# Units of one key block for all heads, loads in order of need, and v cast by DMA, in a fused attention and MLP kernel

## Chip, cores, metric

One core of one Trainium2 chip. The metric is device time in microseconds (us), the median of the runs. "Span" is the length of the one execution that the profiler recorded; it is some 0.3 to 3 us shorter than the median time. Engines are TensorE (PE; its weight loads PEld), VectorE (DVE), ScalarE (ACT), GpSimd (POOL) and SyncE (SP).

## The reference

Eight batches of causal attention with a window of 128 and ALiBi, eight heads of 64, 576 positions; its result is the input of an MLP with ELU (512 to 2048 to 512) over 4608 tokens.

```python
# q, k, v: (8 batches, 8 heads, 576, 64) f32
scores = (1 / 8) * q @ k^T                        # per batch and head
rel = pos_q - pos_k;  slope[h] = 2 ** -(h + 1)    # 8 heads
mask = (rel >= 0) & (rel < 128)
scores = where(mask, scores - slope[h] * abs(rel), -1e9)
attn = softmax(scores);  x = (attn @ v) as (4608 tokens, 512)
h = x @ w_in                                      # w_in (512, 2048)
g = where(h > 0, h, exp(min(h, 0)) - 1)
return g @ w_out                                  # w_out (2048, 512), f32
```

576 is four and a half blocks of 128. Each batch therefore has a last block, called block 4 here, of only 64 positions.

## The kernel before

The MLP is cut into 144 hidden pieces (128 x 512 results each, then ELU on ACT, POOL and DVE) and 144 output pieces (4 matmuls each). A slot of the schedule holds one hidden piece, one output piece and a share of the attention of a later batch. Scores are held transposed (keys on partitions). A unit of attention is half of the heads and half of the positions. Value matmuls of block 4 run on full tiles: columns 512 to 576 of EX, the upper half of key block 4 in VP and the end of KT are zeros.

```python
KT = [one([128, 2, 2, 640], F16, f"KT{i}") for i in range(2)]
EX = [one([128, 4, 576], F16, f"EX{i}") for i in range(4)]
...
for i in range(2):
    V.memset(VP[i][:, :, :, D:D + 1], 1.0)        # gives the softmax's sum
    V.memset(VP[i][64:128, 4, :, 0:D], 0.0)
    V.memset(KT[i][:, :, :, 576:640], 0.0)
for e in EX:
    V.memset(e[:, :, 512:576], 0.0)
...
def values(b, i, h2):
    ...
    parts = {0: [(e0, 0, 0)],
             1: [(e0, 256, 1), (e0, 128, 0)],
             2: [(e1, 0, 2), (e0, 384, 1)],
             3: [(e1, 256, 3), (e1, 128, 2)],
             4: [(e1, 384, 3), (e1, 448, 4)]}[i]
    a = ps_v.tile([128, 4, D + 1], F32, name="av", tag="av")
    for g in range(4):
        for j, (e, c, n) in enumerate(parts):
            nc.tensor.matmul(a[:, g, :], e[:, g, c:c + 128], VP[b % 2][:, n, 2 * g + h2, 0:D + 1],
                             start=j == 0, stop=j == len(parts) - 1)
```

The start: q and k of batch 0 first, then a weight, then v (uncast, by the SP queue, cast by GpSimd), then the other weights and batch 1.

```python
for g in range(4):
    load_qk(0, 1, g); load_qk(0, 0, g)
...
load_wi(0)
for n in range(5):
    load_v(0, n)
load_wi(1)
...
for i in (2, 3):
    load_wi(i)
for g in range(4):
    for w in (1, 0):
        load_qk(1, w, g)
```

The softmax here doesn't subtract the row's maximum and nothing guards it: scores larger than these inputs give would overflow.

Of the kernel before, what the change touches and what calls it, by code (L numbers as in the profile page):

```python
# [14 lines left out]
BIG = 30000.0  # L15
# [3 lines left out]
def kernel(  # L19
# [34 lines left out]
    TAB = one([128, 2, 4, 512], F16, "TAB")  # L54

    QT = [one([128, 2, 2, S], F16, f"QT{i}") for i in range(2)]
    KT = [one([128, 2, 2, 640], F16, f"KT{i}") for i in range(2)]
    VP = [one([128, 5, H, VW], F16, f"VP{i}") for i in range(2)]
    EX = [one([128, 4, 576], F16, f"EX{i}") for i in range(4)]
# [5 lines left out]
    st, vf = {}, {}  # L65
# [8 lines left out]
    def turn_qk(b, w, h2, dh):  # L74
        o = (QT, KT)[w][b % 2][:, h2, dh, 0:S].rearrange("p (n i j) -> p n j i", i=32, j=2)
        V.transpose(o, st[b][:, w, h2, :, :, 32 * dh:32 * dh + 32])  # L76

    def load_v(b, n):
        t = vf[b, n] = stage.tile([128, H, D], F32, name="vf", tag="vf", bufs=5)
        p = 128 if n < 4 else 64  # L80
        if b == 0:
            nc.gpsimd.memset(t[:, 0, 0:1], 0.0)
        nc.sync.dma_start(t[0:p, :, :], v[b, :, 128 * n:128 * n + p, :].rearrange("h p d -> p h d"))

    def cast_v(b, n):
        p = 128 if n < 4 else 64
        nc.gpsimd.tensor_scalar(  # L87
            out=VP[b % 2][0:p, n, :, 0:D], in0=vf.pop((b, n))[0:p, :, :],
            scalar1=1.0, scalar2=0.0, op0=ALU.mult, op1=ALU.add)

    def load_wi(i, n=1):
        c = slice(512 * i, 512 * i + 512 * n)
        nc.gpsimd.dma_start(w_in_sb[:, :, c], moe_w_in[:, c].rearrange("(c p) f -> p c f", p=128))

    def load_wo(i, n=1):
        nc.gpsimd.dma_start(
            w_out_sb[:, 4 * i:4 * i + 4 * n, :],
            moe_w_out[512 * i:512 * i + 512 * n, :].rearrange("(c p) d -> p c d", p=128))
# [3 lines left out]
    with tc.manual_schedule():  # L102


        row = one([128, 1], I32, "row")
        col = one([128, 128], I32, "col")
        rel = one([128, 512], I32, "rel")
        nc.gpsimd.iota(row, pattern=[[0, 1]], base=0, channel_multiplier=1)
        nc.gpsimd.iota(col, pattern=[[1, 128]], base=0, channel_multiplier=0)
        for g in range(4):  # L110
            load_qk(0, 1, g)
            load_qk(0, 0, g)
        for c, n in ((0, 256), (256, 192), (448, 64)):
            nc.gpsimd.iota(rel[:, c:c + n], pattern=[[1, n]], base=0, channel_multiplier=-1)
        load_wi(0)
        for n in range(5):
            load_v(0, n)
        load_wi(1)

        rowf = one([128, 1], F32, "rowf")  # L120
        V.tensor_copy(rowf, row)
        V.tensor_scalar(out=ident, in0=col, scalar1=rowf, scalar2=None, op0=ALU.is_equal)  # L122
        ra = one([128, 512], F32, "ra")
        for i in range(2):
            V.memset(VP[i][:, :, :, D:D + 1], 1.0)
            V.memset(VP[i][64:128, 4, :, 0:D], 0.0)
            V.memset(KT[i][:, :, :, 576:640], 0.0)
        for e in EX:
            V.memset(e[:, :, 512:576], 0.0)
        V.tensor_scalar(out=ra, in0=rel, scalar1=0.0, scalar2=BIG, op0=ALU.is_lt, op1=ALU.mult)  # L130
        V.tensor_tensor(out=ra, in0=ra, in1=rel, op=ALU.add)
        rb = one([128, 512], F32, "rb")
        V.tensor_scalar(out=rb, in0=ra, scalar1=127.0, scalar2=BIG, op0=ALU.is_gt, op1=ALU.mult)
        V.tensor_tensor(out=ra, in0=ra, in1=rb, op=ALU.add)
        for h2 in range(2):
            for g in range(4):
                nc.scalar.activation(TAB[:, h2, g, :], ra, AF.Exp,
                                     scale=-(2.0 ** (-8.0 * (2 * g + h2 + 1) / H)))



        avt, xnt, xps = {}, {}, {}

        def unit(b, k_):
            return EX[(4 * b + k_) % 4]

        def scores(b, k_):
            u, h2 = divmod(k_, 2)
            qt, kt = QT[b % 2], KT[b % 2]
            parts = ([(0, 0, 0, 256), (256, 1, 128, 256)] if u == 0 else  # L150
                     [(0, 2, 256, 256), (256, 3, 384, 192), (448, 4, 512, 64)])
            for o, kb, q0, n in parts:
                for dh in range(2):
                    for g in range(4):
                        r = slice(32 * g, 32 * g + 32)
                        nc.tensor.matmul(  # L156
                            sp[:, g, o:o + n], kt[r, h2, dh, 128 * kb:128 * kb + 128],
                            qt[r, h2, dh, q0:q0 + n], start=dh == 0, stop=dh == 1,
                            tile_position=(32 * g, 0))

        def expo(b, k_, g):
            nc.scalar.activation(unit(b, k_)[:, g, 0:512], sp[:, g, :], AF.Exp, scale=0.125)  # L162

        def weigh(b, k_, gp):
            u, h2 = divmod(k_, 2)
            e = unit(b, k_)[:, 2 * gp:2 * gp + 2, 0:512]
            if u == 0:
                for_ = lambda ap: ap
                e = e.rearrange("p g (a c) -> p g a c", a=2)
                t = TAB[:, h2, 2 * gp:2 * gp + 2, 0:256].unsqueeze(2).broadcast_to([128, 2, 2, 256])  # L170
            else:
                t = TAB[:, h2, 2 * gp:2 * gp + 2, :]
            V.tensor_tensor(out=e, in0=e, in1=t, op=ALU.mult)  # L173

        def values(b, i, h2):
            e0, e1 = unit(b, h2), unit(b, 2 + h2)
            parts = {0: [(e0, 0, 0)],
                     1: [(e0, 256, 1), (e0, 128, 0)],
                     2: [(e1, 0, 2), (e0, 384, 1)],
                     3: [(e1, 256, 3), (e1, 128, 2)],  # L180
                     4: [(e1, 384, 3), (e1, 448, 4)]}[i]
            a = ps_v.tile([128, 4, D + 1], F32, name="av", tag="av")
            for g in range(4):
                for j, (e, c, n) in enumerate(parts):
                    nc.tensor.matmul(a[:, g, :], e[:, g, c:c + 128], VP[b % 2][:, n, 2 * g + h2, 0:D + 1],  # L185
                                     start=j == 0, stop=j == len(parts) - 1)
            if (b, i) not in xnt:
                xnt[b, i] = work.tile([128, 4, 2, D], F16, name="xn", tag="xn", bufs=6)
            r = work.tile([128, 4], F32, name="rden", tag="rden", bufs=2)
            V.reciprocal(out=r, in_=a[:, :, D])  # L190
            V.tensor_tensor(out=xnt[b, i][:, :, h2, :], in0=a[:, :, 0:D],  # L191
                            in1=r.unsqueeze(2).broadcast_to([128, 4, D]), op=ALU.mult)

        def turn(b, i):
            n = 128 if i < 4 else 64
            o = (b * S + 128 * i) % RING
            x = xnt.pop((b, i)).rearrange("p g h d -> p (g h d)")
            if b:
                nc.sync.dma_start_transpose(out=xT[:, :, o:o + n], in_=x[0:n, :])
                return  # L200
            t = ps_o.tile([128, 4, 128], F16, name="xps", tag="op")
            for c in range(4):
                nc.tensor.transpose(t[:, c, :], x[:, 128 * c:128 * c + 128], ident)
            V.tensor_copy(xT[:, :, o:o + n], t[:, :, 0:n])


        hps, es, gs, ops = {}, {}, {}, {}
        width = lambda t: 128 if t < 1 else 256

        def place(t, j):  # L210
            w = width(t)
            sub, s_ = divmod(j, w // 32)
            return w, w * sub, s_ * (512 // w), 512 // w

        def hidden(t, j):
            w, c0, f0, nf = place(t, j)
            p = hps[t, j] = ps_h.tile([128, 512], F32, name="hp", tag="hp")
# [9 lines left out]
            e = es[t, j] = work.tile([128, 512], F32, name="e", tag="e")  # L227
            nc.scalar.activation(e, p, AF.Exp)  # L228
            nc.gpsimd.tensor_scalar(out=e, in0=e, scalar1=1.0, scalar2=0.0, op0=ALU.min, op1=ALU.max)  # L229

        def elu(t, j):
            w, c0, f0, nf = place(t, j)
            if t not in gs:
                gs[t] = gpool.tile([128, NFC, 512], F16, name="g")
            sh = lambda ap: ap.rearrange("p (l c) -> p l c", c=w)
            V.scalar_tensor_tensor(  # L236
                out=gs[t][:, f0:f0 + nf, c0:c0 + w], in0=sh(es.pop((t, j))), scalar=1.0,
                in1=sh(hps.pop((t, j))), op0=ALU.subtract, op1=ALU.max)
# [42 lines left out]
        for g in range(4):  # L281
            at(-4, expo, 0, 0, g)
# [109 lines left out]
```

## Time and profile before

| | before |
|---|---|
| time, median (lowest to highest) | 352.9 us (352.0 to 353.0) |
| span, mean granted clock of TensorE | 350.9 us, 0.976 |
| TensorE busy | 314.4 us, 90% |
| first hidden matmul starts | 34.9 us |
| hidden matmuls waited for ELU; scores for exponentials | 6.5 us; 5.4 us |
| software queue (loads that GpSimd issues), share of the DMA engines | 36.6% |

The lines behind it stand in the prediction. Only TensorE is busy nearly all the time, so read its line first, and the granted clock below it. In the timeline each row is a run of like instructions, with start and length, and in square brackets the idle time before it and what ended it. Ends of matmuls are modelled, so I take costs from **start to start**: the start of the next piece less the start of the hidden piece, less the 0.87 us of that piece.

### The profile page before, as it was taken

Reading aid. Unit: us, or ns where it says so; the run is one execution under the profiler, and the core shown is the slowest. Engines: PE = TensorE matmul, PEld = TensorE weight load, DVE = VectorE, ACT = ScalarE, POOL = GpSimd, SP = SyncE. Lnnn points to the kernel's source line nnn. Section 1 sums busy time; section 2 is a strip of 40 time slices with the busy share of each in tenths; the row PEclk is TensorE's granted clock in tenths of the full one; section 3 lists DMA queues with packets and bytes.
Section 4 is the critical chain, followed back from the end, with each engine's and each line's share of the span. In section 5 each row is a group of like instructions: output and inputs, shape, how many; then the busy total and the mean of one; then the engine's idle time right before and its main releaser. Section 6 shows DMA issues by size and latency. Waiting matters only on the chain.

```text
span 350.9 us, 8428 instructions
## 1 busy us (share of the span) xinstructions
PE 314.4 (90%) x3410; PEld 221.1 (63%) x3410; DVE 236.6 (67%) x453; ACT 176.3 (50%) x317; POOL 169.6 (48%) x270
## 2 busy tenths in 40 slices
PE   8713876889999999899999999999999999999994
PEld 8612756646666666676666666666667667766641
DVE  3804679788769976697669766996689666544420
ACT  1720735645665565546564655465555665344421
POOL 8613465635564545453765456455655222333320
PEclk9985889999999999999999999999999999999999
DMA  9999795894699229921796169823992020310011
GB/s 95 189 189 171 124 170 95 96 212 81 85 129 186 60 56 125 205 78 57 88 199 146 40 81 162 150 69 55 158 180 69 32 60 32 70 60 33 30 60 60
DMA packets 102086, 37.17 MB, mean 106 GB/s; under 512 B 93344, under 2 KB 97440, under 8 KB 102048
## 3 DMA queue, kind: packets, MB, share of 16 engines
q0 software_dynamic: 42112, 13.64, 36.6%
q1 hardware_dynamic: 59936, 23.01, 27.9%
q8 instruction: 26, 0.43, 0.5%
q14 instruction: 12, 0.10, 0.1%
HBM read 36.70 MB, written 9.44 MB: 131 GB/s over the span
## 4 chain that ended last, share of the span: by engine, by line
PE 71%; DVE 8%; DMA 8%; issue 4%; ACT 4%; POOL 3%; ACTq 0%; DVEq 0%; POOLq 0%
PE op L245 32%; PE hp L224 30%; PE sp L156 5%; PE av L185 4%; DMA st<-in_k_dram 4%; DMA wi<-in_moe_w_in_dram 4%; ACT EX L162 3%; DVE g L236 2%; DVE EX L173 2%; POOL st L70 2%; DVE xn L191 1%; DVE KT L76 1%; DVE QT L76 1%; ACT ob L249 1%; POOL e L229 1%
## 5 line engine op out<-in xcount | busy, mean ns | idle before, releaser
L229 POOL TENSOR_SCALAR e<-e 128x512 f32<-128x512 f32 x144 | 95.7, 665 | 147.7 <-ACT e L228 147.2
L224 PE MATMUL hp<-xT,wi 128*128 128x256 f16 (+3 forms) x1408 | 151.5, 255 | 7.1 <-DVE g L236 6.5
L228 ACT ACTIVATE e<-hp 128x512 f32<-128x512 f32 x144 | 86.2, 598 | 129.4 <-PE hp L224 125.0
L224 PEld LDWEIGHTS <-wi 128*128 128x128 f16 x1408 | 120.1, 99 | 49.0 <-issue 11.5
L245 PE MATMUL op<-wo,g 128*128 128x512 f16 x576 | 146.7, 379 | 1.4 <-ACT ob L249 1.4
L236 DVE SCALAR_TENSOR_TENSOR g<-e,hp 128x512 f16<-128x512 f32 x144 | 96.8, 672 | 57.3 <-POOL e L229 57.1
L162 ACT ACTIVATE EX<-sp 128x512 f16<-128x512 f32 x128 | 75.2, 598 | 9.6 <-PE sp L156 9.2
L245 PEld LDWEIGHTS <-g 128*128 128x128 f16 x576 | 49.4, 97 | 42.3 <-issue 4.5
L173 DVE TENSOR_TENSOR EX<-EX,TAB 128x1024 f16<-128x1024 f16 x64 | 49.4, 774 | 1.3 <-ACT EX L162 0.9
L185 PE MATMUL av<-VP,EX 128*128 128x65 f16 x576 | 31.6, 196 | 13.3 <-POOL VP L87 8.5
L185 PEld LDWEIGHTS <-EX 128*128 128x128 f16 x576 | 27.7, 99 | 16.3 <-issue 9.5
L191 DVE TENSOR_TENSOR xn<-av,rden 128x256 f16<-128x256 f32 x80 | 33.9, 424 | 2.8
L190 DVE RECIPROCAL rden<-av 128x4 f32<-128x4 f32 x80 | 14.2, 177 | 29.4 <-PE av L185 28.0
L249 ACT COPY ob<-op 128x512 f32<-128x512 f32 x36 | 21.1, 585 | 23.5 <-PE op L245 23.5
L87 POOL TENSOR_SCALAR VP<-vf 128x512 f16<-128x512 f32 (+1 forms) x40 | 26.3, 659 | 8.8 <-DMA vf<-in_v_dram 8.8
L76 DVE STREAM_TRANSPOSE KT<-st 128x576 f16<-128x576 f16 x32 | 25.9, 817 | 3.4 <-DMA st<-in_k_dram 3.3
L156 PE MATMUL sp<-QT,KT 32*128 32x256 f16 (+2 forms) x640 | 21.1, 255 | 7.8 <-ACT EX L162 5.4
L76 DVE STREAM_TRANSPOSE QT<-st 128x576 f16<-128x576 f16 x32 | 25.7, 811 | 0.0
L70 POOL DMA_DIRECT2D st<-in_k_dram x32 | 22.1, 690 | 6.1 <-DMA wi<-in_moe_w_in_dram 5.6
L70 POOL DMA_DIRECT2D st<-in_q_dram x32 | 21.8, 680 | 5.4 <-DMA wi<-in_moe_w_in_dram 5.4
L156 PEld LDWEIGHTS <-KT 32*128 32x128 f16 x640 | 15.2, 95 | 13.8 <-issue 11.6
L255 PE MATMUL spare<-ident 128*128 128x128 f16 x190 | 13.9, 244 | 1.7 <-DVE ident L122 1.6
(26 smaller groups left out, 37.2 us busy)
## 6 DMA issues: line engine op xcount, KB each, us to landing
out_dram<-ob SPq DMA_DIRECT2D x36, 256.0 KB, 2.2
vf<-in_v_dram SPq DMA_DIRECT2D x32, 256.0 KB, 5.5
st<-in_k_dram POOLq DMA_DIRECT2D x32, 144.0 KB, 3.7
st<-in_q_dram POOLq DMA_DIRECT2D x32, 144.0 KB, 4.7
wi<-in_moe_w_in_dram POOLq DMA_DIRECT2D x4, 512.0 KB, 12.1
wo<-in_moe_w_out_dram POOLq DMA_DIRECT2D x4, 512.0 KB, 8.2
vf<-in_v_dram SPq DMA_DIRECT2D x8, 128.0 KB, 4.9
xT<-xn SPq DMA_TRANSPOSE x35, 2.9
```

Source lines behind the costliest of these rows:

```text
L70: nc.gpsimd.dma_start(st[b][32 * g:32 * g + 32, w, :, :, :, :].rearrange("p h n j d -> p (h n) (j d)"), (q, k)[w][b, 2 * g:2 * g + 2, :, : ...
L76: V.transpose(o, st[b][:, w, h2, :, :, 32 * dh:32 * dh + 32])
L156: nc.tensor.matmul(sp[:, g, o:o + n], kt[r, h2, dh, 128 * kb:128 * kb + 128], qt[r, h2, dh, q0:q0 + n], start=dh == 0, stop=dh == 1, tile_ ...
L162: nc.scalar.activation(unit(b, k_)[:, g, 0:512], sp[:, g, :], AF.Exp, scale=0.125)
L173: V.tensor_tensor(out=e, in0=e, in1=t, op=ALU.mult)
L185: nc.tensor.matmul(a[:, g, :], e[:, g, c:c + 128], VP[b % 2][:, n, 2 * g + h2, 0:D + 1], start=j == 0, stop=j == len(parts) - 1)
L191: V.tensor_tensor(out=xnt[b, i][:, :, h2, :], in0=a[:, :, 0:D], in1=r.unsqueeze(2).broadcast_to([128, 4, D]), op=ALU.mult)
L224: nc.tensor.matmul(p[:, l * w + u0:l * w + u1], w_in_sb[:, c, fc * 128:(fc + 1) * 128], xT[:, c, x0:x0 + u1 - u0], start=(c == 0), stop=(c ...
L228: nc.scalar.activation(e, p, AF.Exp)
L229: nc.gpsimd.tensor_scalar(out=e, in0=e, scalar1=1.0, scalar2=0.0, op0=ALU.min, op1=ALU.max)
L236: V.scalar_tensor_tensor(out=gs[t][:, f0:f0 + nf, c0:c0 + w], in0=sh(es.pop((t, j))), scalar=1.0, in1=sh(hps.pop((t, j))), op0=ALU.subtrac ...
L245: nc.tensor.matmul(ops[t], gs[t][:, fc, ts * 128:(ts + 1) * 128], w_out_sb[:, fc, :], start=(fc == 0), stop=(fc == NFC - 1))
```

## The change

The intent is an earlier and smoother start. q and k of batch 0 are loaded in the order of need and turned by TensorE rather than DVE, with mask and ALiBi added by matmul, so that no table is needed at first. v is cast by its DMA, which takes the casts from GpSimd. A unit is now one key block for all eight heads, spread evenly over the slots; the fill of the pipeline has a schedule of its own. With all heads in one unit there are no spare columns any more, and block 4 gets tiles of its true size. The core of the diff, with cuts marked by dots:

```diff
-    KT = [one([128, 2, 2, 640], F16, f"KT{i}") for i in range(2)]
+    KT = [one([128, 2, 2, S], F16, f"KT{i}") for i in range(2)]
-    EX = [one([128, 4, 576], F16, f"EX{i}") for i in range(4)]
+    EX = [one([128, 4, 2, 256], F16, f"EX{i}") for i in range(4)]
...
+    def load_v(b, n):
+        p = 128 if n < 4 else 64
+        nc.gpsimd.dma_start(VP[b % 2][0:p, n, :, 0:D],
+                            v[b, :, 128 * n:128 * n + p, :].rearrange("h p d -> p h d"))
...
+    def turn_first(w, part, half, tag):
...
+                    nc.tensor.transpose(t[64 * hh:64 * hh + 64, x, j, :], s0[r, w, 4 * hh + nh * half + x, j, :],
+                                        ident[r, r])
...
-            V.memset(VP[i][64:128, 4, :, 0:D], 0.0)
-            V.memset(KT[i][:, :, :, 576:640], 0.0)
-        for e in EX:
-            V.memset(e[:, :, 512:576], 0.0)
...
+            if b == 0:                      # mask and ALiBi by matmul, then q and k
...
+                            nc.tensor.matmul(
+                                sp[0:m, g, 256 * h2 + o:256 * h2 + o + n], SI[:, 2 * g + h2, 0:m], RB[:, 0:n],
+                                start=part == h2 == 0, stop=False, skip_group_check=True)
...
+        def values(b, i, gp):
+            m = 128 if i < 4 else 64
+            parts = ([(unit(b, 3), 128, 3, 128), (unit(b, 3), 192, 4, 64)] if i == 4 else
+                     [(unit(b, i), 0, i, 128)] + ([(unit(b, i - 1), 128, i - 1, 128)] if i else []))
+            a = ps_v.tile([128, 2, 2, D + 1], F32, name="av", tag="av")
+            for g in range(2):
+                for h2 in range(2):
+                    for j, (e, c, n, kk) in enumerate(parts):
+                        nc.tensor.matmul(
+                            a[0:m, g, h2, :], e[0:kk, 2 * gp + g, h2, c:c + m],
+                            VP[b % 2][0:kk, n, 4 * gp + 2 * g + h2, 0:D + 1],
+                            start=j == 0, stop=j == len(parts) - 1)
...
+        load_first(1, 0)
+        load_first(0, 0)
...
+        load_v(0, 0)
+        load_v(0, 1)
+        load_first(1, 1)
+        load_first(0, 1)
+        load_wi(0)
+        load_wi(1)
+        for n in (2, 3, 4):
+            load_v(0, n)
+        load_wi(2)
+        load_wi(3)
...
-        HID = {m + (LAG if m >= 16 else 0): divmod(m, 16) for m in range(16 * NTB)}
-        OUT = {13 + m: divmod(m, 16) for m in range(16 * NTB)}
-        START = [None, 5, 21, 37, 55, 73, 91, 109]
+        for s, (sub, f) in enumerate(first):               # 16 pieces of 128 columns
+            HID[s] = (0, 128 * sub, 128, 4 * f, 4)
+        for f in range(2):
+            HID[16 + f] = (1, 0, 64, 8 * f, 8)
...                                                         # slots 18 to 33: 16 output pieces
+        for f in range(4):
+            HID[34 + f] = (1, 64, 128, 4 * f, 4)
+            HID[40 + f] = (1, 256, 128, 4 * f, 4)
+            HID[44 + f] = (1, 384, 128, 4 * f, 4)
+        for f in range(2):
+            HID[38 + f] = (1, 192, 64, 8 * f, 8)
...
+                HID[16 * t + 16 + j] = (t, 256 * (j // 8), 256, 2 * (j % 8), 2)
...
+                OUT[16 * t + 26 + j] = (t, j // 4, 4 * (j % 4))
...
+        at(17, load_wo, 2)
...
+        at(20, load_wo, 3)
...
+        START = [None, None, 41, 57, 75, 93, 111, 129]
```

## The prediction

> **What bounds the kernel now.** I read the summary page first, then the stretches of the start, the timeline of the start and of one steady slot, the table of waits, and the chain that ended last. TensorE is busy nearly everywhere except in the first sixth of the span, and there its granted clock falls to half:
>
> ```profile
> PE 314.4 (90%) x3410; PEld 221.1 (63%) x3410; DVE 236.6 (67%) x453; ACT 176.3 (50%) x317; POOL 169.6 (48%) x270
> PE   8713876889999999899999999999999999999994
> PEclk9985889999999999999999999999999999999999
> ...
> 15.00:20.00 5.00, 3.75 (x71) 3.33 (x69) 2.85 (x5) 3.75 (x8) 1.11 (x2) 1.00 1.22 196
> 20.00:25.00 5.00, 0.00 (x0) 0.00 (x0) 0.00 (x0) 0.00 (x0) 0.87 (x2) 0.91 1.27 190
> 25.00:30.00 5.00, 0.98 (x12) 0.68 (x11) 1.06 (x4) 0.00 (x0) 2.01 (x4) 0.50 1.47 171
> ```
>
> In the stretches the columns after the width are PE, PEld, DVE, ACT, POOL, then clock, DMA share, GB/s: from 20 to 25 us no compute engine works, only DMA. The timeline says what is awaited: the first value matmul waits for the cast of v on GpSimd, which stood in its queue behind the loads of weights and of batch 1.
>
> ```profile
> 16.23 0.67 POOL L70 DMA_DIRECT2D st<-in_k_dram  x1 [2.85 <-DMA wi<-in_moe_w_in_dram]
> ...
> 26.99 1.21 POOL L87 TENSOR_SCALAR VP<-vf 128x512 f16<-128x512 f32 x2
> 27.68 0.38 PE L185 MATMUL av<-VP,EX 128*128 128x65 f16 x4 [8.54 <-POOL VP L87]
> ...
> 34.89 1.91 PE L224 MATMUL hp<-xT,wi 128*128 128x128 f16 x16
> 36.84 0.60 ACT L228 ACTIVATE e<-hp 128x512 f32<-128x512 f32 x1 [17.38 <-PE hp L224]
> 37.52 0.61 POOL L229 TENSOR_SCALAR e<-e 128x512 f32<-128x512 f32 x1 [4.00 <-ACT e L228]
> 38.16 0.69 DVE L236 SCALAR_TENSOR_TENSOR g<-e,hp 128x512 f16<-128x512 f32 x1 [2.61 <-POOL e L229]
> ```
>
> GpSimd had eight loads in flight when it stopped and issued one more each time one landed. So the first MLP matmul starts at 34.9 us. The ELU chain behind it (ACT, POOL, DVE) takes 2.1 us from the end of the matmuls to the freed bank, and there are two banks. In the middle, one slot holds one hidden piece, one output piece and a share of attention:
>
> ```profile
> 95.59 1.04 PE L224 MATMUL hp<-xT,wi 128*128 128x256 f16 x8
> 96.97 0.62 PE L156 MATMUL sp<-QT,KT 32*128 32x256 f16 x24 [0.34 <-ACT EX L162]
> 97.53 1.04 PE L245 MATMUL op<-wo,g 128*128 128x512 f16 x4
> ...
> 315.98 0.86 PE op L245 x4
> 316.84 0.87 PE hp L224 x8
> ```
>
> The last two lines, from the chain, give the dense cost: 0.87 us for either piece. There are 144 of each, so **250 us is the matmul floor of the MLP**, untouched by the change. A score unit of 24 matmuls costs more than its 0.62 us: the hidden piece started at 95.59 and needs 0.87, the next piece starts at 97.53, so 1.07 us, of which 0.34 waits for the exponentials of the unit before. A unit of 16 measured in the same way costs 0.84. Eight value matmuls cost 0.24.
>
> **What the Trainium skill says.** (1) "TensorE: Matmul & The Clock Gate", Part 1: the array clock is halved after an idle window of about 3.4 us and comes back after as long a busy one. The trace agrees: idle from 19.4 to 27.7 us, clock 0.50 from 25 us. (2) Part 4 of that page warns that transposes do not count as busy; the trace before has too few of them (20) to tell, and the change adds many. (3) "DMA: Bandwidth & Descriptors", SWDGE vs HWDGE vs iDMA: a cast in a DMA can only be issued from GpSimd. The trace agrees as far as it goes: the casting loads are all on the software queue, v comes uncast by the SP queue and is cast by a GpSimd instruction. (4) The same page, Specifications, gives about 358 GB/s of HBM per core. From 8 to 28 us the software queue wrote 2.91 MB, from twice as many bytes read, and the other queue 0.79 MB: 6.6 MB in 20 us, 331 GB/s, so the start is close to that limit, and order of loads matters more than their number. The 0.2 us of idle seen ahead of the score matmuls, which no page is needed for, stays after the change.
>
> **The change, part by part. The start.** q and k of batch 0 come in two row ranges, the first 384 rows of each (0.79 MB apiece read) ahead of all else, then two blocks of v, the rest of q and k, then weights. The first data moved at 2.8 us before. At 300 GB/s (3 to 8 us of the trace: 150 GB/s written, cast to half) k and q part one land by 8.0 us. The two v blocks are 2048 packets of 256 bytes; by bytes 1.7 us, by the packet rate of the first 8 us (2807 packets in 5.2 us) 3.8 us: 9.7 to 11.8. The rest of q and k 2.6 us: 12.3 to 14.4. First weights, 1.05 MB, 3.4 us: 15.7 to 17.8, second 3.4 us later. The eight-in-flight limit now falls on loads that are wanted at that point anyway.
>
> TensorE after the 90 warm-up matmuls (79 ns each before, so until 8.7 us): 96 transposes of 64 columns in four groups, which I put at 50 ns a pair from the value pairs' 40 ns (0.31 us of weight loads for 8) and more for small tiles: 4.8 us, 13.5. The last q copy on ACT, 768 elements, about 0.9 us from 585 ns for 512: 14.5; the 8 mask matmuls (256 columns, 0.11 us each) hide beside it. Scores 0.8: 15.3. Exponential 0.6, value matmuls, reciprocal 0.18 and product 0.42: 17. Meanwhile 96 small transposes, 3.8 us, 20.2; second half of the values; masks 0.9 and scores 0.7, 21.9; exponentials 1.1, next values, turn: **first MLP matmul at about 23.5 us instead of 34.9**, 11.4 us earlier. It waits on no cast and no table.
>
> **The fill.** Now 18 hidden pieces of 128 or 64 columns run before any output piece (before, 13). The two banks allow one each (0.9+2.1)/2 = 1.5 us; PE work in these slots is 16 x 0.89 + 2 x 1.3 = 16.8 us and the rest of batch 0's attention. That is 8 us: two units with masks and scores at 1.7 to 1.9 us (before 0.9), values 2, four turns 1.6. Walking the slots by hand, with the first nine at about 1.95 us and the others at 1.5, outputs begin near 54 us, with some 6 us of TensorE idle. Then 16 output pieces in a row, 13.9 us, with the first units of batch 1: a score unit must wait for an exponential that is queued behind an output copy (0.6 + 0.6 us), 2 us idle in all. Then 8 hidden pieces without output, 1 us idle. The 64-column pieces (32 matmuls at about 41 ns, 1.3 us instead of 0.87, six pieces in all) cost 2.5 us that did not exist before.
>
> **The steady part.** Per batch both kernels have 80 score and 72 value matmuls, 16 exponentials, 8 products, 8 transposes on DVE. Before: 0.84 + 0.84 + 1.07 + 1.07 plus a few waits = 3.9, and 72 x 0.03 = 2.2: 6.1 us. After: three units of 16 at 0.84 and one of 32 at 1.2 = 3.7, as the exponentials are placed in two slots instead of four and the scores no longer wait: 5.9. Seven batches gain about 1.5 us. The casts leave GpSimd (26.3 us busy), but 40 v loads are issued there, at 0.7 to 0.9 us each: no gain, and at 48% busy no harm. DVE has one turn, one product or one reciprocal-and-product per slot besides the ELU step (0.67 + 0.81 + 0.77 = 2.25 us in the worst slots, slot 2.05), where before some slots had all of them (2.85); perhaps 1 us less idle.
>
> **The sum.** Before: start 34.9 + MLP 250 + rest of batch 0 5 + seven batches 42.7 + end 5.1 (two output copies that hold the single bank, 0.7 each, and the last copy and store, 3.7) = 337.7; the span is 350.9, so 13 us are idle or slow-clock time between 35 us and the end. After: 23.5 + 250 + 8 + 41.3 + 2.5 + 5.1 = 330.4, and idle 6 + 2 + 1 + 2 (steady) = 11: span 341.4. Whole runs are 2.0 us above the span before (352.9 against 350.9), so 343.4, **343 us, 2.8% faster**. So of 11.4 us won at the start, about 5 are paid back in masks and narrow pieces, 2 to 3.5 come from fewer waits.
>
> **Rivals.** *A: the start is shortened as above, but the fill gives it all back*: attention of batch 1 starts later against the outputs (at the start of token block 2 the old kernel has batch 2 done, the new one only begins it), so the saved time is owed to later slots. The 250 us floor and the 26 slots with no output beside the hidden piece speak for it; that the old fill idled as well speaks against. It makes 348 to 351. *B: transposes in TensorE do not hold the clock, or are slow*: 192 pairs at 80 ns instead of 45 and a half clock until 25 us put the first MLP matmul at 28: 347. The warm-up directly ahead speaks against. *C: small v packets on the software queue*: 36,864 more packets of 256 bytes read and 128 written; if they halve the queue's rate, weights and batch 1's q and k come late, and DVE, which takes its work in order, stops in a turn: 346 to 352. The loads are issued 8 slots ahead of use, which speaks against. *D: the even placement does more than I count*: most steady waits vanish and the fill is denser: 335 to 338. The table of waits has 6.5 us of hidden matmuls waiting for the ELU step and 5.4 us of scores waiting for exponentials to win from.
>
> **Range and chances.** D with a start at 22 us gives 335; A or B gives 348 to 351. I take 335 to 350. The line for 2% faster is 345.8, 3 us above my value; A, B and C lie beyond it, each with perhaps one chance in eight. Faster 0.62, same 0.34, slower 0.04.
>
> **What would show each step.** First hidden matmul at 22 to 25 us (B: above 27); clock 1.00 throughout (B: halves before 25 us). No wait of value matmuls on GpSimd. Hidden pieces 1.5 to 2 us apart until about 54 us, waits of hidden matmuls on the ELU step grown well above 6.5 us. Score matmuls' wait on exponentials below 3 us after 100 us. Software queue share up from 36.6%, DVE waits on q and k loads under 3 us (C: over 5). Steady slots near 2.0 us, and the last hidden matmul ending as far before the end (14 us) as before. The prediction is wrong if the first hidden matmul comes on time and the end does not (A), or if the idle time in the fill is not there (D).

## The result

| | before | after |
|---|---|---|
| time, median of 4 runs | 352.88 us (351.99 to 352.97) | 361.44 us (360.57 to 361.88) |
| ratio | | 1.0245 (1.0217 to 1.0274) |
| span, granted clock | 350.9 us, 0.976 | 358.8 us, 0.99 |

A ratio is the mean time of one kernel's fast runs over that of the other's of the same rounds, so not quite the ratio of the medians quoted; the interval is 95%. The change makes the kernel **2.5% slower**; predicted was 2.8% faster.

The page of the kernel after, busy times and slices:

```profile
PE 332.8 (93%) x3706; PEld 230.7 (64%) x3706; DVE 223.3 (62%) x443; ACT 175.4 (49%) x313; POOL 172.8 (48%) x261
...
PE   8898879856999999999999999999999999999994
...
PEclk9879999999999999999999999999999999999999
...
q0 software_dynamic: 76480, 18.36, 60.2%
```

The hole in the third and fourth slices is gone, and the clock is higher; a smaller hole is new in the ninth and tenth (72 to 90 us), and the runs f2 to h1 come back to it. Yet TensorE is busy 18.4 us longer, with 3706 matmuls for 3410: the loss is not only waiting, but more work or work that takes longer. Which work, the groups of instructions by shape say. First the value matmuls of before, then those of after (busy time, mean ns of one, idle time ahead), then, from the page of after, all of them in one row:

```profile
L185 PE MATMUL av<-VP,EX 128*128 128x65 f16 x576 | 31.6, 196 | 13.3 <-POOL VP L87 8.5 <-DVE xn L191 2.6 <-DVE EX L173 1.9
```

```profile
L189 PE MATMUL av<-VP,EX 128*128 128x65 f16 x448 | 24.6, 195 | 2.5 <-ACT EX L173 1.3 <-ACT ob L251 0.7 <-DVE xn L198 0.4
L189 PE MATMUL av<-VP,EX 128*64 128x65 f16 x64 | 13.9, 218 | 0.0
L189 PE MATMUL av<-VP,EX 64*64 64x65 f16 x64 | 13.7, 214 | 0.0
```

```profile
L189 PE MATMUL av<-VP,EX 128*128 128x65 f16 (+1 forms) x576 | 44.4, 200 | 2.5 <-ACT EX L173 1.3
```

The pair after the operands is the tile, rows by columns. Busy time counts an overlapped stretch once, so the 128 small matmuls occupy 44.4 - 24.6 = 19.8 us, nearly as much as the 448 full ones. The mean of one hardly shows it, 214 to 218 ns against 195: it is a latency, and matmuls overlap. Busy time per matmul is 55 ns for full ones (24.6 / 448) and 155 ns for small ones. Within one small shape it is the latency itself (13.9 us / 64 = 217 ns): no two of the same shape overlap.

The timeline of TensorE in the kernel before, then of the kernel after, in a steady stretch:

```profile
117.59 1.04 PE L224 MATMUL hp<-xT,wi 128*128 128x256 f16 x8
118.46 0.40 PE L185 MATMUL av<-VP,EX 128*128 128x65 f16 x8
118.70 1.03 PE L245 MATMUL op<-wo,g 128*128 128x512 f16 x4
```

```profile
126.50 1.04 PE L225 MATMUL hp<-xT,wi 128*128 128x256 f16 x8
127.47 1.24 PE L189 MATMUL av<-VP,EX 128*64 128x65 f16 x8
128.64 1.04 PE L247 MATMUL op<-wo,g 128*128 128x512 f16 x4
```

Before, a group of eight costs 118.70 - 117.59 - 0.87 = 0.24 us. After, a group of block 4 costs 128.64 - 126.50 - 0.87 = **1.27 us**. (The row's tile is that of its first matmul; the eight are both kinds.) There are 16 such groups, two per batch: 16 x 1.03 = 16.5 us. The chain that ended last, of the kernel after, runs through them, so this cost is in the time:

```profile
126.67 0.87 PE hp L225 x8
127.54 1.17 PE av L189 x8
128.71 0.97 PE op L247 x4
```

The start, meanwhile, came out better than predicted. The timeline of TensorE in the first microseconds of the kernel after, then one stretch (PE, PEld, DVE, ACT, POOL, clock, DMA share, GB/s):

```profile
8.16 1.71 PE L115 MATMUL tp<-ident,s 64*64 64x64 f16 x96
...
12.32 1.88 PE L115 MATMUL tp<-ident,s 32*64 32x32 f16 x96
...
18.12 1.90 PE L225 MATMUL hp<-xT,wi 128*128 128x128 f16 x16
```

```profile
16.00:18.00 2.00, 1.42 (x16) 0.74 (x13) 0.42 (x1) 1.39 (x2) 0.00 (x0) 0.50 2.16 165
```

The first hidden matmul starts at 18.1 us, 16.8 us earlier than before, though the clock is halved around it (0.50 from 16 to 20 us, and 1.00 again from 22 us). So 16.8 us are won at the start and the end comes 7.9 us later: some 25 us are to be found. The small tiles would be 16.5 of them.

### The profile page after: what moved, and what is told of

It is laid out like the page before. It is cut to its first block, busy times and chain, and to the rows that moved or that the text cites. A ratio compares the mean times of both kernels' runs of the same rounds, so it can differ in the third digit from the quotient of the medians.

```text
span 358.8 us, 8891 instructions
## 1 busy us (share of the span) xinstructions
PE 332.8 (93%) x3706; PEld 230.7 (64%) x3706; DVE 223.3 (62%) x443; ACT 175.4 (49%) x313; POOL 172.8 (48%) x261
## 3 DMA queue, kind: packets, MB, share of 16 engines
q0 software_dynamic: 76480, 18.36, 60.2%
## 4 chain that ended last, share of the span: by engine, by line
PE 68%; DVE 10%; ACT 8%; DMA 4%; issue 4%; POOL 4%; ACTq 0%; DVEq 0%; POOLq 0%
PE hp L225 26%; PE op L247 25%; PE av L189 9%; DVE g L238 5%; ACT EX L173 5%; PE sp L167 4%; POOL e L231 3%; ACT e L230 3%; DMA wo<-in_moe_w_out_dram 2%; DMA out_dram<-ob 2%; PE spare L257 2%; DVE EX L179 2%; DVE KT L127 1%; PE sp L148 1%; DVE QT L127 1%
## 5 line engine op out<-in xcount | busy, mean ns | idle before, releaser
L173 ACT ACTIVATE EX<-sp 128x512 f16<-128x512 f32 (+1 forms) x121 | 69.8, 634 | 15.9 <-PE sp L167 10.1
L179 DVE TENSOR_TENSOR EX<-EX,TAB 128x1024 f16<-128x1024 f16 x56 | 39.1, 699 | 29.5 <-ACT EX L173 29.5
L189 PE MATMUL av<-VP,EX 128*128 128x65 f16 (+1 forms) x576 | 44.4, 200 | 2.5 <-ACT EX L173 1.3
L189 PEld LDWEIGHTS <-EX 128*128 128x128 f16 (+1 forms) x576 | 34.7, 100 | 12.6 <-issue 3.1
L198 DVE TENSOR_TENSOR xn<-av,rden 128x256 f16<-128x256 f32 (+1 forms) x80 | 33.8, 423 | 2.7
L93 POOL DMA_DIRECT2D VP<-in_v_dram x40 | 35.0, 879 | 0.7 <-issue 0.6
L197 DVE RECIPROCAL rden<-av 128x4 f32<-128x4 f32 (+1 forms) x80 | 14.1, 176 | 24.1 <-PE av L189 23.9
L127 DVE STREAM_TRANSPOSE KT<-st 128x576 f16<-128x576 f16 x28 | 22.5, 814 | 0.0
L87 POOL DMA_DIRECT2D st<-in_q_dram x28 | 19.1, 681 | 2.7 <-DMA wo<-in_moe_w_out_dram 2.1
L167 PEld LDWEIGHTS <-KT 32*128 32x128 f16 (+1 forms) x560 | 10.5, 95 | 5.9 <-issue 4.2
L257 PE MATMUL spare<-ident 128*128 128x128 f16 x90 | 6.6, 249 | 1.6 <-DVE ident L282 1.6
```

The lines of the kernel that those rows point to most:

```text
L87: nc.gpsimd.dma_start(st[b][32 * g:32 * g + 32, w, :, :, :, :].rearrange("p h n j d -> p (h n) (j d)"), (q, k)[w][b, 2 * g:2 * g + 2, :, : ...
L93: nc.gpsimd.dma_start(VP[b % 2][0:p, n, :, 0:D], v[b, :, 128 * n:128 * n + p, :].rearrange("h p d -> p h d"))
L127: V.transpose(o, st[b][:, w, h2, :, :, 32 * dh:32 * dh + 32])
L167: nc.tensor.matmul(sp[0:m, g, 256 * h2 + o:256 * h2 + o + n], kt[r, h2, dh, 128 * kb:128 * kb + m], qt[r, h2, dh, q0:q0 + n], start=dh == ...
L173: nc.scalar.activation(unit(b, u)[:, g0:g1, :, c0:c1], sp[:, g0:g1, :].rearrange("p g (h c) -> p g h c", h=2)[:, :, :, c0:c1], AF.Exp, sca ...
L179: V.tensor_tensor(out=e, in0=e, in1=TAB[:, int(u == 3), 2 * gp:2 * gp + 2, :, :], op=ALU.mult)
```

## The experiments

My first theory: the tiles of block 4 cost about 16 us, because TensorE must empty itself between tiles of different shape. The Trainium skill has it in "TensorEngine Tiling (Array Packing)", Key Properties: "Mode switching requires drain". It gives no cost. The rivals: small matmuls are slow in themselves; the small packets of v on the software queue slow the rest (C of the prediction); the fill gives back what the start won (A).

The ratio column is to the kernel before, in the same rounds; before took 352.7 to 352.9 us in all of them.

| run | built on | time, us | ratio (95%) | span |
|---|---|---|---|---|
| e1_full_tile | after | 346.09 | 0.980 (0.976 to 0.984) | 345.6 |
| e2_grouped | after | 349.14 | 0.990 (0.987 to 0.994) | 347.6 |
| e3_before_small | before | 366.20 | 1.038 (1.035 to 1.041) | 364.5 |
| e4_v_uncast | after | 361.41 | 1.026 (1.022 to 1.030) | 359.2 |
| m1_rows_same | e1 | 348.60 | 0.988 (0.985 to 0.991) | 348.3 |
| m2_cols_same | e1 | 359.74 | 1.019 (1.014 to 1.023) | 358.1 |
| f2_fill_waits | e1 | 341.59 | 0.968 (0.966 to 0.971) | 340.4 |
| f3_fill_banks | f2 | 338.39 | 0.959 (0.957 to 0.962) | 337.4 |
| g1_order_undone | e1 | 355.91 | 1.010 (1.005 to 1.014) | 353.3 |
| b1_order_only | before | 351.15 | 0.996 (0.992 to 1.001) | 348.3 |
| h1_lag | f3 | 332.26 | 0.943 (0.940 to 0.946) | 331.8 |

All gave correct results.

### e1_full_tile: block 4 on full tiles

```diff
-    EX = [one([128, 4, 2, 256], F16, f"EX{i}") for i in range(4)]
+    EXW = [one([128, 2048 + 64], F16, f"EX{i}") for i in range(4)]
+    EX = [t[:, 0:2048].rearrange("p (g h c) -> p g h c", g=4, h=2) for t in EXW]
...                                          # in values; the masks of key block 4 also get 128 partitions
+                        if i == 4:
+                            o = 512 * (2 * gp + g) + 256 * h2 + c
+                            nc.tensor.matmul(
+                                a[:, g, h2, :], EXW[3][:, o:o + 128],
+                                VP[b % 2][:, n, 4 * gp + 2 * g + h2, 0:D + 1],
+                                start=j == 0, stop=j == len(parts) - 1)
+                            continue
...
+            V.memset(VP[i][64:128, 4, :, 0:D], 0.0)
+        V.memset(EXW[3][:, 2048:2112], 0.0)
```

> The changed kernel with the value matmuls of the last query block (64 rows) done on the full 128x128 tile for both parts, as the kernel before did: same number of matmuls, results of the 64 spare columns left unread. Theory 1 (those 128 matmuls alternate between a 128x64 and a 64x64 tile and each alternation costs a drain; a group of 8 costs 1.27 us instead of 0.24, sixteen groups): 16 us less, so about 345 us. Theory 2 (the loss sits in the fill or in DMA, and the extra busy time of these matmuls is a record's artefact): 359 to 362.

Measured 346.09 us, 15.3 us less than after. The same amount of matmuls, of more rows and columns, is faster. The group of the kernel e1:

```profile
L192 PE MATMUL av<-VP,EX 128*128 128x65 f16 x128 | 6.5, 193 | 0.0
```

19.8 us of busy time became 6.5, and a group costs 0.24 us again (125.89 - 124.78 - 0.87 in its timeline). Without this one detail the change is 2.0% faster than before; its interval includes 2%, so whether it is over 2% stays unclear. The scores of key block 4 were cut to their true size as well (112 matmuls on 32x64 tiles); e1 leaves that, and no run undid it. It adds one change of tile to one score unit of each later batch.

### e2_grouped: the same small tiles, in another order

```diff
-            for g in range(2):
-                for h2 in range(2):
-                    for j, (e, c, n, kk) in enumerate(parts):
+            heads = [(g, h2) for g in range(2) for h2 in range(2)]
+            turns = ([(g, h2, j) for j in range(2) for g, h2 in heads] if i == 4 else
+                     [(g, h2, j) for g, h2 in heads for j in range(len(parts))])
+            for g, h2, j in turns:
...
-                            start=j == 0, stop=j == len(parts) - 1)
+                    start=j == g == h2 == 0 if i == 4 else j == 0, stop=j == len(parts) - 1,
+                    skip_group_check=i == 4)
```

> The changed kernel with the same tiles (128x64 and 64x64) in the last query block, but the four first parts of a group ahead of the four second parts, so two changes of tile per group instead of eight. Theory 1a (the alternation costs): a group falls from 1.27 to about 0.5 us, 12 us less, about 349 us. Theory 1b (a 64-column tile itself is slow, whatever the order): no change, 361 us.

Measured 349.14 us. The groups of the kernel e2:

```profile
L191 PE MATMUL av<-VP,EX 128*64 128x65 f16 x64 | 5.0, 200 | 0.0
L191 PE MATMUL av<-VP,EX 64*64 64x65 f16 x64 | 5.0, 197 | 0.0
```

The same 128 matmuls, ordered as four first parts and then four second parts (only the start flag differs with that), are busy 5.0 us in each shape rather than 13.9 and 13.7. A group costs 124.74 - 123.29 - 0.87 = 0.58 us. So small matmuls are **not slow in themselves**; alternating them is. This rival is out.

### e3_before_small: the small tiles alone, in the kernel before

```diff
+            m = 128 if i < 4 else 64
...
-                    nc.tensor.matmul(a[:, g, :], e[:, g, c:c + 128], VP[b % 2][:, n, 2 * g + h2, 0:D + 1],
+                    kk = 64 if n == 4 else 128
+                    nc.tensor.matmul(a[0:m, g, :], e[0:kk, g, c:c + m], VP[b % 2][0:kk, n, 2 * g + h2, 0:D + 1],
```

> The kernel before with only this one part of the change: the value matmuls of the last query block on 128x64 and 64x64 tiles, alternating. Theory 1: sixteen groups of 8 at 1.0 us more each, nearly all on TensorE's path: 14 to 17 us more than the kernel before, 367 to 370. Theory 2: same as the kernel before, 353.

Measured 366.2 us, 13.5 us more than before. The cost appears without any other part of the change (the reciprocal, the product and batch 0's transposes of block 4 are narrowed with it; that is cut above). The expectation, 367 to 370, is missed by 0.8 us, and 13.5 is under the 16.5 of the sum. A group that lies where TensorE waits anyway would cost less: behind the first one in e3's timeline stands a wait of 0.72 us for DVE. For the rest this is not shown.

### m1_rows_same and m2_cols_same: which change of shape

m1 keeps e1's rows and halves the columns; m2 keeps the columns and halves the rows of the second part.

```diff
-                                a[:, g, h2, :], EXW[3][:, o:o + 128],
+                                a[0:64, g, h2, :], EXW[3][:, o:o + 64],
```

> As e1, but the value matmuls of the last query block write 64 columns: both parts on a 128x64 tile, so within a group of 8 nothing alternates; only the step into and out of the group changes the column tiling. Theory 1a (each change of tile drains): two changes of 0.15 us per group in place of none, sixteen groups: 3 to 5 us above e1, 349 to 351. Theory 1b (64 columns are slow by themselves): most of the 15 us of e1 lost again, 357 to 361.

```diff
-                                a[:, g, h2, :], EXW[3][:, o:o + 128],
-                                VP[b % 2][:, n, 4 * gp + 2 * g + h2, 0:D + 1],
+                                a[:, g, h2, :], EXW[3][0:kk, o:o + 128],
+                                VP[b % 2][0:kk, n, 4 * gp + 2 * g + h2, 0:D + 1],
```

> As e1, but the second part of each head uses only its 64 valid rows: 128x128 and 64x128 tiles alternate, columns never change. If a change of row tiling costs as much as a change of both: 358 to 362. If only the column tiling drains: 346 to 348, as e1.

Measured 348.60 us (m1, 0.4 us below the expected 349 to 351) and 359.74 us (m2, as expected for a cost of rows too). The timeline of TensorE in m1, then in m2:

```profile
125.61 1.04 PE L233 MATMUL hp<-xT,wi 128*128 128x256 f16 x8
126.57 0.44 PE L192 MATMUL av<-VP,EX 128*64 128x65 f16 x8
126.94 1.04 PE L255 MATMUL op<-wo,g 128*128 128x512 f16 x4
```

```profile
127.72 1.04 PE L233 MATMUL hp<-xT,wi 128*128 128x256 f16 x8
128.59 1.14 PE L192 MATMUL av<-VP,EX 128*128 128x65 f16 x8
129.66 1.04 PE L255 MATMUL op<-wo,g 128*128 128x512 f16 x4
```

In m1 the group begins 0.96 us after the hidden piece and not 0.87: a gap of 0.09 us at the change of tile. In m2 the first matmul has the tile of the hidden piece, and no gap, but the changes are within the group. Counting the changes of tile from the hidden piece to the output piece, and the cost above 0.24 us, read in the same way in all (the expectation of e2 counted within the group, two and eight):

| kernel | order of tiles in a group | changes | group, us | extra, us | per change | extra x 16 | time over e1 |
|---|---|---|---|---|---|---|---|
| e1 | all 128x128 | 0 | 0.24 | 0 | | 0 | 0 |
| m1 | all 128x64 | 2 | 0.46 | 0.22 | 0.11 | 3.5 | 2.5 |
| e2 | four 128x64, four 64x64 | 3 | 0.58 | 0.34 | 0.11 | 5.4 | 3.1 |
| m2 | 128x128 and 64x128 in turn | 8 | 1.07 | 0.83 | 0.10 | 13.3 | 13.7 |
| after | 128x64 and 64x64 in turn | 9 | 1.27 | 1.03 | 0.11 | 16.5 | 15.3 |

Each change of tile shape costs **0.10 to 0.11 us**, of rows or of columns, and the sum over 16 groups comes within 2.3 us of the time. The scores, on 32-row tiles, show the same gap: in e1 they start at 123.36 us, behind a group on full tiles that starts at 123.02 and costs 0.24, so 0.10 us late. This agrees with the skill's sentence and adds its size. What in the array takes the time, the trace cannot show.

### e4_v_uncast: v of batches 2 to 7 cast on GpSimd again

```diff
+        if b > 1:
+            t = vf[b, n] = stage.tile([128, H, D], F32, name="vf", tag="vf", bufs=5)
+            nc.sync.dma_start(t[0:p, :, :], v[b, :, 128 * n:128 * n + p, :].rearrange("h p d -> p h d"))
+            return
...
+                at(a - 3 + n, cast_v, b, n)
```

> The changed kernel with v of batches 2 to 7 loaded uncast by the SP queue and cast by GpSimd again, in the same slots. Rival C of the prediction (small casting packets on the software queue slow the loads): 3 to 8 us less. Theory 1: within 1.5 us of the changed kernel, 360 to 363.

Measured 361.41 us, as after (361.44). The share of the software queue fell from 60.2% to 41.1% and the time did not move. Rival C is out for the steady part, and the cast by DMA is worth nothing there either. The v loads of batches 0 and 1, which fall in the start and the fill, stayed as they were; for these C was not tested.

### f2_fill_waits and f3_fill_banks: the fill

With full tiles, e1 starts its hidden pieces 15.8 us earlier than before, and ends only 6.6 us earlier in time (346.1 against 352.7 in the same rounds). Its timeline shows waits in the fill, on TensorE and on ACT:

```profile
59.16 1.89 PE L255 MATMUL op<-wo,g 128*128 128x512 f16 x8 [1.65 <-DMA wo<-in_moe_w_out_dram]
...
72.72 0.59 ACT L259 COPY ob<-op 128x512 f32<-128x512 f32 x1 [2.35 <-DMA out_dram<-ob]
...
73.86 1.04 PE L168 MATMUL sp<-QT,KT 32*128 32x256 f16 x16 [2.64 <-ACT EX L174]
```

Output pieces wait for w_out, which is loaded late (2.2 us in two waits); an output copy waits for a store to free one of three buffers, the exponentials queue behind it on ACT, and the scores wait for those. f2 loads w_out earlier and gives the copies five buffers:

```diff
-                ob = work.tile([128, DO], F32, name="ob", tag="ob")
+                ob = work.tile([128, DO], F32, name="ob", tag="ob", bufs=5)
...
-        at(17, load_wo, 2)
+        at(7, load_wo, 2)
...
-        at(20, load_wo, 3)
+        at(12, load_wo, 3)
```

> e1 with the last two output-weight loads issued at slots 7 and 12 instead of 17 and 20, and five output buffers instead of three. The fill of e1 shows 2.2 us of outputs waiting for those weights and 2.6 us of scores waiting for an exponential behind a copy that waits for a store. If these waits are on the path: 3 to 5 us less than e1, 341 to 343. If something behind them takes over: within 1.5 us of e1.

Measured 341.59 us, 4.5 less than e1. f3, on top of it, gives the hidden pieces of slots 10 to 17 four PSUM banks in turn rather than two, which takes the wait for ELU from them:

```diff
+        for n, s in enumerate(range(10, 18)):
+            HID[s] += ((ps_o, "op"), (ps_v, "av"), (ps_h, "hp"), (ps_h, "hp"))[n % 4]
```

> f2, and hidden pieces of slots 10 to 17 cycle over four PSUM banks instead of two. If the two banks set the 1.58 us per piece there: pieces come every 1.0 us, 3 to 5 us less than f2, 337 to 340. If the ELU chain or the loads of weights do: within 1.5 us of f2.

Measured 338.39 us, 3.2 less than f2. Over the whole kernel the waits of hidden matmuls on ELU fell from 10.3 us (f2) to 6.5 us; eight pieces in a row now take 6.7 us (40.43 to 47.16 in f3's timeline), where f2 has one each 1.58 us.

### g1_order_undone and b1_order_only: what the order of loads is worth

g1 is e1 with all weights ahead of v. (It is not quite the order of the kernel before: there v itself came by the SP queue, and only its casts stood behind the other loads.)

```diff
-        load_v(0, 0)
-        load_v(0, 1)
         load_first(1, 1)
         load_first(0, 1)
-        load_wi(0)
-        load_wi(1)
-        for n in (2, 3, 4):
+        for i in range(4):
+            load_wi(i)
+        for n in range(5):
             load_v(0, n)
-        load_wi(2)
-        load_wi(3)
```

> e1 with the order of the first loads undone: all of q and k of batch 0, then the four weight loads, then v, as the kernel before had it (v stays a casting load). If order of need is what brings the first hidden matmul from 34.9 to 18 us: it falls back to 28 to 31 us, and 8 to 12 us of it reach the end, 354 to 358. If the transposes and the missing cast do it: within 3 us of e1, 345 to 349.

Measured 355.91 us. The timeline of TensorE in g1:

```profile
22.04 0.38 PE L197 MATMUL av<-VP,EX 128*128 128x65 f16 x4 [9.30 <-DMA VP<-in_v_dram]
...
29.46 1.05 PE L233 MATMUL hp<-xT,wi 128*128 128x128 f16 x16
```

The first hidden piece comes 10.4 us later than in e1 (29.46 against 19.09 us), and the end 9.8 us later. Here nearly all that is lost at the start is lost at the end. Without the order, the rest of the change, on full tiles, is 1% slower than before, although its first hidden piece is 5.4 us earlier.

b1 is the reverse, the order alone in the kernel before:

```diff
+        load_v(0, 0)
+        load_v(0, 1)
         for g in range(4):
...
-        for n in range(5):
+        for n in range(2, 5):
             load_v(0, n)
...
+        for i in (2, 3):            # after the casts of v, in the schedule
+            at(-3, load_wi, i)
+        for g in range(4):
+            for w in (1, 0):
+                at(-2, load_qk, 1, w, g)
```

> The kernel before with only its loads put in order of need: the first two blocks of v ahead of q and k, the second half of the input weights and batch 1's q and k behind the casts. If the order is the larger share: first hidden matmul at 22 to 26 us, clock not halved, and 6 to 10 us less, 343 to 347. If the old transposes and casts hold it back: above 349.

Measured 351.15 us: **missed**, no difference from before. The timeline of b1:

```profile
19.86 0.62 POOL L87 TENSOR_SCALAR VP<-vf 128x512 f16<-128x512 f32 x1 [8.80 <-DMA vf<-in_v_dram]
...
29.83 0.66 POOL L70 DMA_DIRECT2D st<-in_k_dram  x1 [3.08 <-DMA wi<-in_moe_w_in_dram]
...
33.03 1.20 POOL L231 TENSOR_SCALAR e<-e 128x512 f32<-128x512 f32 x2
...
34.43 1.87 PE L226 MATMUL hp<-xT,wi 128*128 128x128 f16 x16 [2.24 <-DVE g L238]
```

The first hidden piece is at 27.49 us, 7.4 us earlier than before, and not at 22 to 26. I had forgotten that the casts of v blocks 2 and 3, for whose loads GpSimd waits 8.8 us, stand on the same queue ahead of the remaining weight loads and of the ELU step. The last two loads of batch 1 then wait for weights to land (3.08 us at 29.83, 1.86 at 32.35), and GpSimd's share of the ELU of the first two hidden pieces runs only behind them, at 33.03. So hidden pieces wait for ELU in a half-speed clock (0.60 from 25 to 30 us, 0.50 to 40), and the gain is lost. In the kernel before this order does not pay; in e1 it does. That the casts are what makes the difference fits the timeline, but no run took them alone out of the kernel before.

### h1_lag: outputs nearer to their hidden pieces

f3, with the outputs of token blocks 1 to 8 three slots earlier, so that the slots after the fill have an output piece to run while hidden ones wait, and with the last block's outputs in two banks in turn:

```diff
-                OUT[16 * t + 26 + j] = (t, j // 4, 4 * (j % 4))
+                OUT[16 * t + 23 + j] = (t, j // 4, 4 * (j % 4)) + (
+                    (ps_v, "av") if t == NTB - 1 and j // 4 % 2 else ())
```

> f3 with the output pieces of blocks 1 to 8 three slots nearer to their hidden pieces and the last block's outputs alternating over two banks. The stretch of hidden pieces without output (slots 34 to 41) then has three outputs in its idle time, and the end loses two waits of 0.7 us: 2 to 4 us less than f3, 334 to 336. If the ELU chain is then awaited by outputs: no gain, 338.

Measured **332.26 us**, the fastest version: 5.7% faster than before, 8% faster than the change as given, and below the 334 to 336 that I expected. The stretch after the fill, in e1 and then in h1 (PE, PEld, DVE, ACT, POOL, clock, DMA share, GB/s):

```profile
69.90:103.20 33.30, 26.15 (x441) 20.87 (x441) 25.80 (x53) 18.34 (x34) 16.63 (x24) 0.95 0.85 94
```

```profile
70.00:100.00 30.00, 27.32 (x425) 20.09 (x425) 24.59 (x51) 16.61 (x31) 17.15 (x26) 1.00 0.78 84
```

TensorE is idle 7.2 us of 33.3 in e1, and 2.7 of 30 in h1. At the end, the two waits of 0.72 us for the output bank are gone. The two edits were not run apart, so how the 6.1 us over f3 divide stays open, but the second can hardly give more than those 1.4 us. Nor was any of f2, f3 and h1 tried on the kernel before, so how much of the 5.7% they would give there is not known; the change with full tiles alone is e1's 2.0%.

## Why the prediction was wrong

**The step that failed** is in the steady part: "Per batch both kernels have 80 score and 72 value matmuls", and "72 x 0.03 = 2.2". Counted, that is right; but I took the rate of full tiles in an unbroken run for all 72. Sixteen of the 72 alternate between two tile shapes, and each change of shape costs some 0.1 us. The term is 56 x 0.03 + 2 x 1.27 = 4.2 us per batch and not 2.2, by the timeline of after; over eight batches that is some 16 us, of which e1 took 15.3 away. Without it the change takes 346.1 us, 3 us above what was predicted and inside the range. None of the four rivals held it. The diff showed it (`m`, `kk`), and the skill's sentence on the drain stood in a page that I left uncited. The trace before showed a sign too: the idle time ahead of the score matmuls, which have another tile than their neighbours. (How much of those 0.2 us the tile made there was not measured; in e1 it is 0.10.) I put it aside with "stays after the change" and did not ask where else such a change of tile would appear.

**The other steps**, by the list that the prediction gave for checking:

- *Start.* Predicted 23.5 us, measured 18.1. The transposes were over-sized: 96 of 64 columns in 1.71 us, not 4.8, and the 96 small ones in 1.88, not 3.8. g1 shows the order of loads to be worth 10.4 us here. That the loads run close to a limit of HBM (331 of 358 GB/s) was read and not tested.
- *Clock 1.00 throughout.* Wrong: 0.50 from 16 to 20 us. The first half of rival B holds, its delay does not. It fits what the skill says of transposes ("TensorE: Matmul & The Clock Gate", Part 4), but other waits precede it as well, and no run took the transposes out: not shown.
- *No wait of value matmuls on GpSimd.* Right; 8.5 us of it are gone.
- *Outputs begin near 54 us.* They began at 52.2. *Waits on ELU well above 6.5 us:* 9.4, right. The stretch from the first hidden piece took 34.1 us, though, rather than 30.5; two groups of block 4 are some 2 us of that (in e1 it took 31.3). *Narrow pieces:* one takes 0.93 us where nothing waits (51.27 to 52.20), not 1.3, so that six cost some 0.4 us more and not 2.5.
- *Idle in the fill.* Mis-sized. I had 2 us for the 16 output pieces and 1 us for the hidden ones after them. In e1 the outputs took 19.5 us, where I had 15.9 and the first scores of batch 1 apart, and the stretch after them has 7.2 us idle. f2, f3 and h1 got back 13.8 us in all. This made up for the early start, and so the sum came near e1 by errors that cancel, which is luck. (The parts listed for the rest of batch 0 add up to 7.0 to 7.4 us, not to 8; 1.05 MB at 300 GB/s take 3.5 us, not 3.4; TensorE's idle time began at 19.1 us, not 19.4. None of these matters for the result.)
- *Scores' wait on exponentials below 3 us.* Right: 2.7 us, none of it after 100 us. *Queue share up, waits of DVE on q and k small:* right, 60.2% and 0.7 us; e4 confirms for the steady part that it costs nothing.
- *Steady slots near 2.0 us.* Wrong for two slots in each batch: the chain shows 3.01 us for them (126.67 to 129.68).
- *Last hidden matmul as far before the end:* 15.3 us, before 14.2; about right.

**Rivals.** A holds by half: of 15.8 us won at the start, e1 keeps 6.6 at the end. B holds for the clock alone. C is excluded for the steady part. D holds only with edits that the change did not have.

## What to carry to other kernels

Don't cut a matmul down to its valid rows or columns when its neighbours have another tile: pad with zeros to one tile shape, or at least group by shape, and count each change of shape as about 0.1 us of TensorE here. Look for it by the busy time per matmul in the groups by shape, not by the mean length, which hid it (155 against 55 ns of busy time each, but 216 against 195 in the mean). Time won at the start reaches the end only if the pipeline's fill has buffers, banks and weights early enough to take it; read that stretch by itself.

## What the Trainium skill lacked or had wrong

- "TensorEngine Tiling (Array Packing)", Key Properties, is right that a change of tiling mode drains TensorE, but has no size for it: 0.10 to 0.11 us per change in four orders of tiles here, and the same for a change of rows as of columns.
- The same page, When to Use Tiling, recommends row tiling for a contraction of 64 or less without a word on neighbours with other tiles. Here, alternating 64-row tiles with full ones cost 13.7 us over e1 (m2), and with 128x64 ones 15.3 us (after); the latter grouped cost 3.1 us (e2).
- "TensorE: Matmul & The Clock Gate", Part 4, gives about 275 ns for a 128 x 128 transpose in a kernel, and no rate for a row of small ones. As the length of one it fits (255 ns for the 128 x 128 ones of the kernel before); but 96 of 64 x 64, each 193 ns long, passed in 1.71 us, 18 ns each. Its remark that transposes do not count as busy fits the clock of 0.50 some microseconds later, but no run isolated it.
